# Nine products of a zeroed tile, x and a table asked for in another order, and the first filter pairs signed and turned elsewhere in a filter-and-experts kernel

## The chip, the cores and the metric

The kernel runs on one core of one Trainium2 chip. Its time is device time in microseconds, from five executions: the median is 475.29 (473.47 to 477.4). A sixth execution was taken with the hardware profiler; views of it are called the profile or the trace. The engines are PE (TensorE: matmuls and transposes), DVE (VectorE), ACT (ScalarE), POOL (GpSimd) and SP (SyncE, which here only issues DMAs). ACT and POOL issue DMAs too.

## The reference

What is computed, cut to what matters:

```python
# x: (8, 2496, 256); filt_r, filt_i: (1249, 256)
X = np.fft.rfft(x, axis=1)
y = np.fft.irfft(X * (filt_r + 1j * filt_i)[None], n=2496, axis=1)
t = y.reshape(19968, 256)                       # tokens
logits = t @ w_gate                             # 8 experts
expert = logits.argmax(1); p = softmax(logits)  # the gate of a token is p of its expert
out = zeros
for e in range(8):                              # the 80 tokens of highest gate are kept
    keep = top 80 of the tokens with expert == e
    out[keep] = gate[keep] * (relu(t[keep] @ w1[e]) @ w2[e])
```

## The kernel before, in words

The real transform of length 2496 = 39 x 64 is done as matrix products in float32, one sequence after another. Sequences are numbered b = 0 to 7.

- `load_x(b, ch)` (line 293) brings a chunk of x, 468 KB (the last of a sequence 234 KB), six chunks to a sequence, by SP's queue into one of NX0 = 7 buffers. Number 6b + ch gives the order of the chunks; chunk n takes the buffer of chunk n - 7, so its load waits until stage 1 has read that one.
- `stage1(b, k)` (302), eleven blocks k to a sequence, two blocks to a chunk: products with the table `wf_t` on PE into a PSUM tile `pa` (L309), copied by ACT into `t1` (L315). Here a block is 8 PE instructions in the profile.
- `transpose1(b, u)` (317), u = 0 to 9: four transposes of `t1` into `pt` (L323), copied by ACT to `t2` (L325). It needs all of the sequence's `t1`.
- `stage2(b, u)` (329): products with piece u // 2 of the table `d_t` into `pb` (L334); DVE multiplies by the two halves of the filter, `ft[0]` and `ft[1]` (two L342), POOL adds and subtracts the parts (two L348).
- `turn(b, u)` (352): products with `gi`, which holds an identity and the gate weights, into `py` (L357); ACT copies the spectrum out (L373) and stores it every second time (`yf`), DVE adds up the gate part `z` (L379, L380).

The filter is brought once, in ten rows of pairs: `load_filter(v, half)` (268) issues two indirect DMAs on POOL (L271), real part (half 0) or imaginary part (half 1) of pair v, v = 0 to 4. The row list `frow` is loaded by ACT's queue at the start. `sign_filter(v)` (276) turns the sign of imaginary rows on ACT (two L279), `turn_filter(v, k)` (282) transposes four tiles of half k on PE into a PSUM tile `pf` (L287), and DVE copies it into `ft[k]` (L289). `ft` of pair v serves the stage 2 of steps 2v and 2v + 1.

PSUM is dealt out in rings: `fps` has three buffers that `pa`, `pt` and `pb` take in turn; `pkps` has one buffer, in which `pf` lies; `yps` has two for `py`. A tile waits until the buffer's last reader is done.

The order of the work is written out by hand (lines 791 to 907): each engine and each queue runs its own instructions in the order in which this part of the program emits them, and waits only for data, for buffers and, for a DMA, for earlier landings. It emits

1. the loads of `frow`, `wf_t`, `fsig` by ACT's queue; on SP's queue the six chunks of sequence 0, piece 0 of `d_t` (`load_d(0)`), the first chunk of sequence 1; on POOL the gathers of filter pair 0, fills of zeros, the identities of `gi`, a copy `mark` of one element of the last chunk of sequence 0 (L826), which makes POOL wait for that chunk, then the gathers of pairs 1 and 2, with the gate weights (two small DMAs, L828 and L829) between the halves of pair 1;
2. eleven blocks of stage 1 of sequence 0; after each finished chunk the next load of x is issued (`put_x` in `put_s1`), and pieces 1 to 3 of `d_t` after blocks 2, 5 and 8;
3. the signing of pair 0, both its halves turned, `transpose1` of steps 0 and 1, each with a block of sequence 1, then piece 4 of `d_t`;
4. steps v = 0 to 81, v = 10b + u: `stage2(v)`; in steps 0 to 7 the signing (odd v) and turning of half v % 2 of pair v // 2 + 1; gathers of pairs 3 and 4 in steps 0 to 3; `transpose1` of step v + 2; a block of stage 1 (two where u = 3); a store of zeros to the output from step 10 on; `turn` of step v - 2.

After the last step come the gathers of the chosen tokens' rows, the choice itself, and the experts' two layers with their weights.

Of the kernel before, what the change touches and what calls it, by code (L numbers as in the profile page):

```python
# [13 lines left out]
F32 = mybir.dt.float32  # L14
BF16 = mybir.dt.bfloat16
# [8 lines left out]
B, S, C = 8, 2496, 256  # L24
# [3 lines left out]
NU = NS // 2  # L28
# [4 lines left out]
NCH = -(-NG // JC)  # L33
# [3 lines left out]
E, FF = 8, 1024  # L37
NDB, NFC = C // 128, FF // 128
# [43 lines left out]
def kernel(  # L82
# [11 lines left out]
    nc = tc.nc  # L94
# [9 lines left out]
                                  name=f"rows{h}_tbl") for h in range(2)]  # L104
# [5 lines left out]
    consts = ctx.enter_context(tc.tile_pool(name="consts", bufs=1))  # L110
    dpool = ctx.enter_context(tc.tile_pool(name="dram", bufs=1, space=DRAM))

    ident = consts.tile([128, 128], F32, name="ident")
    make_identity(nc, ident)
    ident_bf = consts.tile([128, 128], BF16, name="ident_bf")
# [63 lines left out]


    NE, NY, NO = 3, 2, 3
    yf = {b: dpool.tile([128, NS, C], F32, name=f"yf_{b}") for b in range(B)}
    ypool = ctx.enter_context(tc.tile_pool(name="spec", bufs=NY))
    ysb = {}
# [49 lines left out]
    with ExitStack() as actx:  # L234
# [6 lines left out]
        NX0 = 7  # L241
# [4 lines left out]
        fps = pool("fps", 3, PSUM)  # L246
        yps = pool("yps", 2, PSUM)
        pkps = pool("pkps", 1, PSUM)
# [12 lines left out]
        gi = tpool.tile([128, 2, ZW], F32, name="gi")  # L261
        ft = [tpool.tile([128, NU, NDB, 2, NQ], F32, name=f"ft{i}") for i in range(2)]

        st = {}
# [11 lines left out]
        def sign_filter(v):  # L276
            f = fst[:, v]
            for i in range(2):
                nc.scalar.activation(out=f[:, 2 + i, :], in_=f[:, 2 + i, :], func=AF.Copy,  # L279
                                     scale=fsig[:, 2 * v + i:2 * v + i + 1])  # L280

        def turn_filter(v, k):
            f = fst[:, v]
            ps = pkps.tile([128, 2, NDB, 128], F32, name=f"pf_{k}_{v}", tag="k")
            for i in range(2):
                for cb in range(NDB):
                    nc.tensor.transpose(ps[:, i, cb, :],  # L287
                                        f[:, 2 * k + i, 128 * cb:128 * cb + 128], ident[:])
            nc.vector.tensor_copy(  # L289
                out=ft[k][:, 2 * v:2 * v + 2].rearrange("p u c s q -> p u c (s q)"),  # L290
                in_=ps[:])

        def load_x(b, ch):
            xt = xpool.tile([128, JC, C], F32, name=f"x_{b}_{ch}", tag="x")
            ng = min(JC, NG - JC * ch)
            nc.sync.dma_start(
                out=xt[0:NJ * N1, 0:ng, :],
                in_=bass.AP(tensor=x.tensor, offset=x.offset + (b * S + JC * ch) * C,
                            ap=[[N2 * C, N1], [(NG - 1) * C, NJ], [C, ng], [1, C]]))
            st["x", b, ch] = xt  # L300
# [491 lines left out]
        with tc.manual_schedule():  # L792
            nc.scalar.dma_start(out=frow, in_=frow_dram.ap())
            nc.scalar.dma_start(out=wf_t, in_=wf_dram.ap())
            nc.scalar.dma_start(out=fsig, in_=fsig_dram.ap())
            xs = [(b, ch) for b in range(B) for ch in range(NCH)]
            s1 = [(b, k) for b in range(B) for k in range(NB)]

            def put_x():
                if xs:  # L800
                    load_x(*xs.pop(0))

            def put_s1():
                if s1:
                    b, k = s1.pop(0)
                    stage1(b, k)
                    if (2 * k + 2) % JC == 0 or k == NB - 1:
                        put_x()

            def load_d(g):  # L810
                nc.sync.dma_start(out=d_t[:, SG * g:SG * g + SG, :],
                                  in_=d_dram.ap()[:, SG * g:SG * g + SG, :])

            for _ in range(NCH):
                put_x()
            load_d(0)
            for _ in range(NX0 - NCH):
                put_x()
            load_filter(0, 0)
            load_filter(0, 1)  # L820
            for t in (lg, zero_t, *zs, key, kt):
# [1 line left out]
            nc.gpsimd.tensor_copy(out=gi[:, 0, 0:128], in_=ident[:])  # L823
            nc.gpsimd.tensor_copy(out=gi[:, 1, 0:128], in_=ident[:])
            mark = tpool.tile([1, 1], F32, name="mark")
            nc.gpsimd.tensor_copy(out=mark[:], in_=st["x", 0, NCH - 1][0:1, 0, 0:1])  # L826
            load_filter(1, 0)
            nc.gpsimd.dma_start(out=gi[:, 0, 128:128 + E], in_=moe_w_gate[0:128, :])  # L828
            nc.gpsimd.dma_start(out=gi[:, 1, 128:128 + E], in_=moe_w_gate[128:256, :])  # L829
            load_filter(1, 1)  # L830
            load_filter(2, 0)
            load_filter(2, 1)
            for k in range(NB):
                put_s1()
                if k in (2, 5, 8):
                    load_d(k // 3 + 1)
            sign_filter(0)
            turn_filter(0, 0)
            turn_filter(0, 1)
            for v in range(LEAD):  # L840
                transpose1(0, v)
                put_s1()
            load_d(4)
            nlow = max(128 - cap, 8) // 8
            n0 = max(128 - cap, 8) // 8
            early = {67: [lambda: pick_edge(0, 6, 8, -1.0)],
# [17 lines left out]
            for v in range(B * NU + LATE):  # L864
                b, u = divmod(v, NU)
                if b < B:
                    stage2(b, u)
                    if v + 2 < NU:
                        if v % 2 == 1:
                            sign_filter(v // 2 + 1)  # L870
                        turn_filter(v // 2 + 1, v % 2)
                    if v < 4:
                        load_filter(3 + v // 2, v % 2)
                    elif v == 4:
                        nc.gpsimd.dma_start(out=e_t, in_=e_dram.ap())
                        nc.gpsimd.dma_start(out=wi_t, in_=wi_dram.ap())
                    w = v + LEAD
                    if w < B * NU:
                        transpose1(*divmod(w, NU))
                    put_s1()  # L880
                    if u == 3:
                        put_s1()
                    if b > 0:
                        put_zeros(1)
                if v >= LATE:
                    turn(*divmod(v - LATE, NU))
                if b > 0 and u == LATE:
                    logits(b - 1, 0)
                if b > 0 and b % 2 == 0:
                    if u == LATE + 1:  # L890
                        logits(b - 1, 1)
                    if b < 6 and u in (4, 5, 6, 7, 8, 9):
                        gating(b // 2 - 1, u - 4)
                        if u == 9:
                            gating(b // 2 - 1, 6)
                    elif b == 6 and u in (4, 5):
                        gating(2, 2 * u - 8)
                        gating(2, 2 * u - 7)
                    elif b == 6 and u in (6, 7):
                        gating(2, u - 2)  # L900
                        if u == 7:
                            gating(2, 6)
                for act in early.pop(v, []):
                    act()
                if v == B * NU + 1:
                    turn_rows(0, 0)
                    turn_rows(0, 1)
# [663 lines left out]
```

## Time and profile before

| | us |
|---|---|
| median of five executions | 475.29 |
| lowest, highest | 473.47, 477.4 |
| the profiled execution | 474.33 |
| its span, first to last instruction | 472.5 |
| PE busy in 0:20, 20:40, 40:60, 60:80 of the span | 12.84, 15.72, 19.62, 20.00 |
| ACT busy in the same stretches | 10.95, 11.11, 13.49, 13.62 |
| DVE busy | 3.05, 9.12, 10.20, 9.18 |
| POOL busy | 11.21, 16.65, 10.70, 8.48 |
| share of the DMA engines' time in use | 0.81, 0.91, 0.61, 0.66 |

A line of a view names the start and length in us (in the timeline), the engine, the line of the kernel, the operation, the tiles written <- read, the shape, and how many of them were merged (x8). In square brackets stands how long the engine sat idle before it and what ended that. In the table of waits a line reads: who waited <- for whom: us in total, times, longest. PEld is PE's loading of weights, which overlaps its products.

### The profile page before, as it was taken

What the parts mean: (1) busy time and instruction counts of PE and PEld (TensorE: products, weight loads), DVE (VectorE), ACT (ScalarE), POOL (GpSimd) and SP (SyncE); (2) the same over time, 40 slices, a digit from 0 to 9 for tenths busy, and PEclk for the clock granted to TensorE, in tenths of its full rate; (3) what the DMA queues carried; (4) which work ended last, traced back from release to release, by engine and by line L of the source; (5) the groups of instructions that cost most, each with busy time, mean ns of one, the idle gap of its engine ahead of it and who ended that gap; (6) DMA issues with size and microseconds to landing.
All of it is one profiled execution on the core that took longest, in us unless ns stands there. A gap on an engine that the chain in (4) does not pass through costs nothing. (4 is left out here: it accounts for less than half of the span.)

```text
span 472.5 us, 8669 instructions
## 1 busy us (share of the span) xinstructions
PE 433.6 (92%) x3380; PEld 408.2 (86%) x3380; DVE 185.5 (39%) x542; ACT 223.0 (47%) x364; POOL 184.2 (39%) x252
## 2 busy tenths in 40 slices
PE   4879999999999999999999998999939999999970
PEld 4769999999999999999999987888838888888850
DVE  2135544454664455664437984385200000110000
ACT  3747666666776766666667553322212231111110
POOL 7488343443543433543434549204560002113110
PEclk9999999999999999999999999999988999999995
DMA  7998467888778787788962225987857953998010
GB/s 200 255 268 273 132 193 250 243 253 251 263 235 254 272 279 242 206 275 259 388 258 83 104 120 192 362 323 291 326 171 305 378 207 104 376 389 294 7 28 2
DMA packets 39476, 109.95 MB, mean 233 GB/s; under 512 B 5073, under 2 KB 14608, under 8 KB 38658
## 3 DMA queue, kind: packets, MB, share of 16 engines
q1 hardware_dynamic: 28688, 76.41, 49.5%
q10 hardware_dynamic: 6178, 21.04, 11.3%
q0 software_dynamic: 4560, 11.86, 8.2%
q8 instruction: 29, 0.48, 0.4%
q14 instruction: 21, 0.17, 0.1%
HBM read 68.97 MB, written 43.20 MB: 237 GB/s over the span
## 5 line engine op out<-in xcount | busy, mean ns | idle before, releaser
L348 POOL TENSOR_TENSOR p<-p,p 128x256 f32<-128x256 f32 x160 | 114.2, 736 | 134.9 <-DVE p L342 107.2
L342 DVE TENSOR_TENSOR p<-pb,ft 128x512 f32<-128x512 f32 x160 | 102.2, 680 | 15.8 <-PE pb L334 15.7
L315 ACT COPY t<-pa 128x480 f32<-128x480 f32 x88 | 87.1, 1000 | 27.5 <-PE pa L309 27.4
L309 PE MATMUL pa<-wf_t,x 117*128 117x120 f32 x704 | 92.5, 279 | 7.2 <-DMA x<-in_x_dram 6.9
L309 PEld LDWEIGHTS pa<-wf_t,x 117*128 117x128 f32 x704 | 86.5, 195 | 7.6 <-DMA x<-in_x_dram 5.7
L357 PE MATMUL py<-gi,p 128*128 128x136 f32 x640 | 88.1, 280 | 2.3 <-POOL p L348 2.3
L334 PE MATMUL pb<-d_t,t 128*128 128x128 f32 x640 | 85.2, 276 | 0.2
L357 PEld LDWEIGHTS py<-gi,p 128*128 128x128 f32 x640 | 79.8, 190 | 2.9 <-POOL p L348 2.9
L334 PEld LDWEIGHTS pb<-d_t,t 128*128 128x128 f32 x640 | 78.0, 191 | 1.0 <-PE py L357 0.4
L325 ACT COPY t<-pt 128x512 f32<-128x512 f32 x80 | 46.9, 586 | 65.0 <-PE pt L323 64.2
L504 PE MATMUL po<-yb,wt 128*128 128x256 f32 x240 | 58.5, 389 | 7.6 <-issue 6.7
L504 PEld LDWEIGHTS po<-yb,wt 128*128 128x128 f32 x240 | 44.5, 195 | 13.4 <-issue 6.9
L323 PE MATMUL pt<-ident,t 128*128 128x128 f32 x320 | 48.0, 273 | 0.0
L497 ACT COPY wt<-pw 128x512 f32<-128x512 f32 x40 | 23.3, 586 | 52.4 <-PE pw L493 41.1
L379 DVE COPY z<-py 128x16 f32<-128x16 f32 x60 | 11.2, 186 | 91.7 <-ACT ysp L373 57.9
L323 PEld LDWEIGHTS pt<-ident,t 128*128 128x128 f32 x320 | 37.7, 142 | 0.0
L373 ACT COPY ysp<-py 128x512 f32<-128x512 f32 x60 | 35.4, 590 | 0.0
L1147 PEld LDWEIGHTS ph<-xs,w 128*128 128x128 f32 x256 | 29.7, 192 | 1.7 <-DVE xs L1138 1.1
L1147 PE MATMUL ph<-xs,w 128*128 128x80 f32 x256 | 29.8, 274 | 0.8 <-DVE xs L1138 0.8
L1162 PE MATMUL po<-w,hT 128*80 128x256 f32 x128 | 28.8, 379 | 0.0
L1117 POOL DMA_INDIRECT xg<-y_sel,idxg x8 | 7.7, 966 | 45.9 <-DMA y_sel<-yr 44.0
L1167 POOL DMA_INDIRECT out_dram<-ys,idxs x8 | 7.5, 934 | 46.1 <-ACT ys L1165 46.1
(195 smaller groups left out, 331.4 us busy)
## 6 DMA issues: line engine op xcount, KB each, us to landing
out_dram<-zero_t SPq DMA_DIRECT2D x64, 312.0 KB
x<-in_x_dram SPq DMA_DIRECT2D x40, 468.0 KB
w<-in_moe_w_dram SPq DMA_DIRECT2D x16, 1024.0 KB
yf<-ysp ACTq DMA_DIRECT2D x30, 512.0 KB
yb<-yf SPq DMA_DIRECT2D x6, 2560.0 KB
yf<-ys ACTq DMA_DIRECT2D x10, 512.0 KB
x<-in_x_dram SPq DMA_DIRECT2D x8, 234.0 KB
d_t<-d_tbl SPq DMA_DIRECT2D x5, 256.0 KB
```

What stands on the lines that cost most here:

```text
L309: nc.tensor.matmul(out=ps[:, i, :, 2 * NS * cb:2 * NS * cb + 2 * NS], lhsT=xt[0:NJ * N1, (2 * k + i) % JC, 128 * cb:128 * cb + 128], rhs=w ...
L315: nc.scalar.copy(out=t1[:, 2 * k - h:2 * k - h + 2], in_=ps[:])
L323: nc.tensor.transpose(ps[:, i, cb, :], t1[:, a:a + 2, :].rearrange("p r n -> p (r n)"), ident[:])
L325: nc.scalar.copy(out=t2[:].rearrange("p i c -> p (i c)"), in_=ps[:].rearrange("p i c q -> p (i c q)"))
L334: nc.tensor.matmul(out=ps[:, cb, i], rhs=d_t[:, 2 * u + i, :], start=True, stop=True, lhsT=t2[:, i, 128 * cb:128 * cb + 128])
L342: nc.vector.tensor_tensor(out=pt, in0=ps[:].rearrange("p c s r q -> p (c s) r q"), in1=f.unsqueeze(2).to_broadcast([128, 2 * NDB, 2, NQ]), ...
L348: nc.gpsimd.tensor_tensor(out=yt[:, :, r, :], in0=yt[:, :, r, :], in1=pr[1][:, :, 1 - r, :], op=op)
L357: nc.tensor.matmul(out=ps[:, i, ZW * cb:ZW * cb + ZW], rhs=gi[:, cb, :], lhsT=yt[:, 2 * cb + i].rearrange("p r q -> p (r q)"), start=True, ...
L373: nc.scalar.copy(out=dst.rearrange("p s (h w) -> p s h w", h=2), in_=pv[:, :, :, 0:128])
L504: nc.tensor.matmul(pos[t][:, 0, 0:C], lhsT=wts[t, g // 2][:, g % 2, i, :], rhs=ybs[t][:, s, :], start=(s == 0), stop=(s == NS - 1))
L1147: nc.tensor.matmul(ph[:, fc // 4, fc % 4, 0:cap], lhsT=self.w1s[e][:, k, 128 * fc:128 * fc + 128], rhs=xs[:, k, :], start=(k == 0), stop=( ...
L1162: nc.tensor.matmul(po[0:cap, :], lhsT=hT[:, fc, :], rhs=self.w2s[e][:, fc, :], start=(fc == 0), stop=(fc == NFC - 1))
```

## The change

- A tile `warm` of zeros, 128 x 128 in bfloat16, is filled on DVE first of all; nine products of it with itself, 512 columns wide, are put ahead of the first block on PE. They write a tile of the ring `fps` that nobody reads.
- The gate weights are loaded by ACT's queue, right after `fsig`, and no longer by POOL's.
- `mark` reads chunk 3 of sequence 0, no longer chunk 5.
- Pieces 1 to 4 of `d_t` are asked for after block 7 and in steps 0, 2 and 4; a dictionary `held` names for chunks 7 to 20 the step before which they are not asked for (-1: after block 7). This is a place in the order of emission. A chunk is also asked for only when an earlier one has been used up (`free`).
- The signing of pair 0 is emitted after block 6. Before the steps there is one block of sequence 1, not two; the other comes in step 7.
- In steps 0 to 7 the turning of a filter half moves from after `stage2` to after the block of stage 1. The imaginary halves lie in the ring `fps`, not in `pkps`.

```diff
+    warm = consts.tile([128, 128], BF16, name="warm")
+    nc.vector.memset(warm[:], 0.0)
...
+    NWARM = 9
...
         def turn_filter(v, k):
             f = fst[:, v]
-            ps = pkps.tile([128, 2, NDB, 128], F32, name=f"pf_{k}_{v}", tag="k")
+            ps = (fps if k else pkps).tile([128, 2, NDB, 128], F32, name=f"pf_{k}_{v}",
+                                           tag="f" if k else "k")
...
             nc.scalar.dma_start(out=fsig, in_=fsig_dram.ap())
+            for cb in range(NDB):
+                nc.scalar.dma_start(out=gi[:, cb, 128:128 + E],
+                                    in_=moe_w_gate[128 * cb:128 * cb + 128, :])
+            pre = fps.tile([128, 4, 128], F32, name="warm_ps", tag="f")
+            for _ in range(NWARM):
+                nc.tensor.matmul(out=pre[:], lhsT=warm[:], start=True, stop=True,
+                                 rhs=warm[:].unsqueeze(1).to_broadcast([128, 4, 128]))
...
-            def put_x():
-                if xs:
+            held = dict(zip(range(NX0, NX0 + 14),
+                            (-1, 0, 2, 3, 4, 5, 7, 8, 11, 13, 15, 16, 17, 18)))
+            free = [NX0]
+
+            def put_x(v):
+                while xs and free[0] and held.get(B * NCH - len(xs), -1) <= v:
                     load_x(*xs.pop(0))
+                    free[0] -= 1
 
             def put_s1():
                 if s1:
                     b, k = s1.pop(0)
                     stage1(b, k)
                     if (2 * k + 2) % JC == 0 or k == NB - 1:
-                        put_x()
+                        free[0] += 1
...
             for _ in range(NCH):
-                put_x()
+                load_x(*xs.pop(0))
             load_d(0)
             for _ in range(NX0 - NCH):
-                put_x()
+                load_x(*xs.pop(0))
+            free[0] = 0
...
-            nc.gpsimd.tensor_copy(out=mark[:], in_=st["x", 0, NCH - 1][0:1, 0, 0:1])
+            nc.gpsimd.tensor_copy(out=mark[:], in_=st["x", 0, NCH - 3][0:1, 0, 0:1])
             load_filter(1, 0)
-            nc.gpsimd.dma_start(out=gi[:, 0, 128:128 + E], in_=moe_w_gate[0:128, :])
-            nc.gpsimd.dma_start(out=gi[:, 1, 128:128 + E], in_=moe_w_gate[128:256, :])
             load_filter(1, 1)
...
             for k in range(NB):
                 put_s1()
-                if k in (2, 5, 8):
-                    load_d(k // 3 + 1)
-            sign_filter(0)
-            turn_filter(0, 0)
-            turn_filter(0, 1)
+                if k == 6:
+                    sign_filter(0)
+                if k == 7:
+                    load_d(1)
+                    put_x(-1)
+            for k in range(2):
+                turn_filter(0, k)
             for v in range(LEAD):
                 transpose1(0, v)
-                put_s1()
-            load_d(4)
+            put_s1()
...
                     stage2(b, u)
-                    if v + 2 < NU:
-                        if v % 2 == 1:
-                            sign_filter(v // 2 + 1)
-                        turn_filter(v // 2 + 1, v % 2)
+                    if v + 2 < NU and v % 2 == 1:
+                        sign_filter(v // 2 + 1)
+                    if v in (0, 2, 4):
+                        load_d(2 + v // 2)
+                    put_x(v)
...
                     put_s1()
-                    if u == 3:
+                    if u == 3 or v == 7:
                         put_s1()
+                    if v + 2 < NU:
+                        turn_filter(v // 2 + 1, v % 2)
```

## The prediction

> **What bounds the kernel now.** The page comes first: its busy table, then its 40 slices (11.8 us each).
>
> ```profile
> PE 433.6 (92%) x3380; PEld 408.2 (86%) x3380; DVE 185.5 (39%) x542; ACT 223.0 (47%) x364; POOL 184.2 (39%) x252
> ...
> PE   4879999999999999999999998999939999999970
> DMA  7998467888778787788962225987857953998010
> ```
>
> TensorE (PE) is full from slice 4 to slice 24, so until about 283 us the time is PE work plus the holes in the first 60 us. DMA is full in slices 2 and 3 and nearly idle (2) in slices 22 to 24, so no backlog is carried out of the main loop: what the start gains, the loop's end gains, and all later work hangs on that end. Next the PE timeline of the start:
>
> ```profile
> 5.66 5.63 PE L309 MATMUL pa<-wf_t,x 117*128 117x120 f32 x32 [5.66 <-DMA x<-in_x_dram]
> 11.56 2.02 PE L309 MATMUL pa<-wf_t,x 117*128 117x120 f32 x16 [0.27 <-ACT t L315]
> 14.81 4.85 PE L309 MATMUL pa<-wf_t,x 117*128 117x120 f32 x40 [1.24 <-DMA x<-in_x_dram]
> ...
> 21.08 0.83 PE L287 MATMUL pf<-ident,fst 128*128 128x128 f32 x4 [0.98 <-ACT fst L279]
> ```
>
> A block of stage 1 is 8 of these. Blocks 0 to 3 run from 5.66, 4 and 5 from 11.56, 6 to 10 from 14.81: the last two groups start when a chunk of x lands. The table by windows counts 18 products in the 3.80 us from 5.66 (0.211 us each), 16 in the 1.84 us after that (0.115). Its clock column reads 1.00 in both, but the spacing shows a PE at about half rate until 9.46. Third, the waits of PE from 15 to 60 us, and the stall at 28:
>
> ```profile
> PE pf L287 <- ACT fst L279: 2.5, 5, 1.0
> PE pf L287 <- issue: 2.1, 1, 2.1
> PE pa L309 <- DMA x<-in_x_dram: 1.2, 1, 1.2
> ```
> ```profile
> 19.35 0.95 POOL L271 DMA_INDIRECT fst<-in_filt_r_dram,frow  x1 [0.30 <-issue]
> ...
> 23.11 0.98 POOL L271 DMA_INDIRECT fst<-in_filt_i_dram,frow  x1 [0.30 <-issue]
> ...
> 28.00 0.44 PE L287 MATMUL pf<-ident,fst 128*128 128x128 f32 x2 [2.07 <-issue]
> ```
>
> After 19.67 PE waits for filters, not for x: for their signing on ScalarE (ACT), and at 28.00 for a gather issued at 19.35, 8.65 us earlier. Last, a step without a stall:
>
> ```profile
> 50.09 1.05 PE L334 MATMUL pb<-d_t,t 128*128 128x128 f32 x8
> 50.98 0.60 PE L287 MATMUL pf<-ident,fst 128*128 128x128 f32 x4
> 51.41 0.60 PE L323 MATMUL pt<-ident,t 128*128 128x128 f32 x4
> 51.85 1.05 PE L309 MATMUL pa<-wf_t,x 117*128 117x120 f32 x8
> 52.74 1.10 PE L357 MATMUL py<-gi,p 128*128 128x136 f32 x8
> 53.67 1.05 PE L334 MATMUL pb<-d_t,t 128*128 128x128 f32 x8
> ```
>
> From start to start: stage 2 0.89, a filter half 0.44, transposes 0.44, a block 0.89, the turn back 0.93; together 3.59.
>
> **The change, part by part.**
>
> *Nine products.* Before shows no bf16 product 512 wide. Below, one costs what a 120-wide one does, 0.211, so nine take 1.9; above, 512/120 x 0.211 = 0.90, so nine take 8.1. From about 1.2 us they end between 3.1 and 9.3. Even at 9.3 blocks 0 to 5 end by 14.9 (six at 0.92), when block 6 may start now. Their gain, were x there, is 3.80 x (1 - 0.115/0.211) = 1.7 us. But chunks 2 and 3 still open their groups at 11.56 and 14.81, since these loads are issued as before and first on SP's queue. I take 0, and keep -1.7 and +0.2. The memset (a like one on POOL takes 0.20) lies on an idle DVE.
>
> The Trainium skill, "TensorE: Matmul & The Clock Gate", Part 1, says that the clock doubles after a busy window of some 3.4 us; nine cold products of 512 columns at 1.2 GHz are an estimate of 3.8 us, enough. By the rule alone the sum would be 1.7 lower; the row of x's arrival says that this is waiting time.
>
> *Gate weights to ACT's queue.* POOL loses two issues, 20.31 to 21.50 and the gap to 21.80: 1.5 us between two gathers. ACT issues them instead (0.6 each) before its table load at 2.17; its first copy is at 7.75, so 0. If that cover went, 1.3.
>
> *The mark.* It waits for chunk 3 of x (PE takes it up at 14.81) and not chunk 5 (17.73): gathers of filter pair 1 start 3.0 us earlier (15.05, 16.3), its second half 4.2 (17.6, 18.9), later ones 4.2.
>
> *Signing pair 0 after block 6.* ACT copies blocks 6 to 10 back to back, 4.76 us from 15.97. Adding 0.89 there ends the last at 21.62, and the transposes, which need it, start at 21.65 instead of 21.75. So the PE wait of 0.98 becomes a wait for ACT: gain 0.1. Bounds: 0, and 0.98 if ACT catches up. Then transposes, one block, and stage 2 of step 0 at 23.4; before it was 24.40 with one block more (0.89), so 23.51 like for like.
>
> *SP's order.* Table pieces go ahead of x of sequence 1; nothing in the trace ties an SP issue to a step, only to a free buffer (136.0 us of waits on L309) or to an earlier landing (6.7 us). The chunk after d piece 1 is needed at 27.6 rather than 28.71; before it was queued ahead of that piece. The earlier gathers share with it: DMA gives 265 GB/s here; gathers of 131 KB, issued one per 1.27 us, can take up to 103 of it, so the 0.74 MB up to and with the chunk of block (1,0) take 0.74/0.162 = 4.6 us from 17.7: 22.3, needed at 22.5. I take 0; bounds -0.5 and +1.5.
>
> *Filters turned last in a step, imaginary halves in the ring `fps`.* Without stalls steps 0 to 7 are 2 x 2.66 + 4 x 3.59 + 2 x 4.48 = 28.6 with the block moved into step 7, 27.7 as before. Before took 57.85 - 24.40 = 33.45: 5.7 lost. What is late next:
> - pair 1 real: 16.3 + 8.65 = 25.0, turned at 25.65: hidden, 0.7 to spare.
> - pair 1 imaginary: the gather at 23.11 is signed at 31.48, 8.4 later; now 18.9 + 8.4 = 27.3, signed by 27.8, turned at 28.8: hidden. Behind the signing on ACT stand the copies of transposes and block.
> - later pairs: POOL does two gathers and two L348 in 4.0 us per step (29.19 to 32.99 to 36.82: 3.8); PE needs 3.6 to 4.9. They keep the 1 to 2 us to spare.
> - new wait: the ring has 3 buffers. In odd steps the imaginary half (or, in 3 and 7, the second block) takes the buffer that stage 2 filled three tiles before. DVE frees it after its two L342, 2.4 to 2.6 us after stage 2 began (37.22 to 39.67: 2.45), and PE is there after 2.22. So 0.3 in steps 1 and 5, 0.45 in 3 and 7 where DVE also has `z` to add, and 0.2 at the start of step 1: 1.7 in all. The turn back and the next stage 2 are queued behind it. Bounds: 0 and 3.0.
>
> Loop: 5.7 - 1.7 = 4.0. **Sum: 4.0 + 0.1 = 4.1 us.** The profiled execution took 474.33 (span 472.5, 1.8 outside): 470.2. The median, 475.29, lies 0.96 above it: 471.2.
>
> What lies behind should move as a whole: SP's wait of 50.6 us on L342 for a spectrum ends with the loop. A stretch at clock 0.83 (340 to 360 us) may fall otherwise, 20 x 0.17 = 3.4 us at most, which is luck of either sign.
>
> The skill's "DMA: Bandwidth & Descriptors", Queues, rings and completion order, has each DMA engine take turns between queues by packet, so gathers issued earlier slow the x transfers beside them. The sum above has that by the trace's own rates; by the rule with equal turns SP would have half of 265, that chunk would land at 23.3, and 0.8 of the gain would go.
>
> **The rivals.**
> - *More comes back*: DVE keeps up, the ring costs nothing (1.7 more), and ACT or x come a little earlier (0.7). Gain 6.5: 468.8. For it: DVE is busy 10.2 of 20 us in 40:60. Against: it stands behind ACT in `z` (57.9 us of waits).
> - *The filters stay late*: 2.0 us more from issue to use, since x, table and eight gathers now ask together. Steps 0 and 1 stall again: gain 2.0, 473.3, no change that can be told. For it: DMA at 0.91 in 20:40. Against: no byte is added.
> - *Slower, by x of sequence 2*: chunks 15 to 18 are asked for two steps (6.4 us) ahead of use in SP's order, where before it was eleven. If SP really stands at its step, behind zero stores and landings, and a chunk needs 8 us (as the gathers do), five chunks cost 1.6 each, 8.0, less 4.1: 479.2. It decides once issue to landing exceeds 6.4 us at 65 to 95 us. Against: DMA there is at 0.64 to 0.86, and SP waits for nothing of a step.
> - *Not what it says*: the clock is not released by the nine products. By the sum above the time is then the same, so its chance is in the forecast's.
>
> **How the numbers follow.** A measurement here tells 0.5% (2.4 us) from no change: 472.9 to 477.7 is the same. Forecast 471.2 (469.8 to 472.9): 0.57. More comes back: 0.19. Late filters: 0.15. Slower: 0.09. Faster is 0.57 + 0.19 = 0.76. The range leaves out the slower case and the outer edges of both neighbours: 468.0 to 474.2.
>
> **What would show it.** Right: products at 0.115 from the first x on, blocks 6 to 10 still opened near 14.8; step 0's stage 2 near 23.4; no hole before L287 at 25 to 31; stage 2 of step 8 near 53.8 instead of 57.85; small holes before L287 or L309 in odd steps, released by L342. Wrong: a wait of L309 on x after 20 us, POOL's L348 or ACT before PE in steps 0 to 7, or a tail that does not follow the loop's end.

## The result, and the profile after

The changed kernel takes 475.19 us (median of 43 runs, 469.53 to 478.24), the kernel before 476.11 (85 runs, 472.44 to 479.48): a ratio of 0.9965, 95% interval 0.9952 to 0.9979. The ratio compares executions in the faster of two states alone, so it is not the quotient of these medians. It stands for 1.7 us, less than the 0.5% that the prediction called no change. The forecast was 471.2, its range 468.0 to 474.2: wrong. The profiled execution of after took 475.36, with a span of 473.5; that of before, 474.33, lies 1.8 under its median here, so the two traces side by side show the places, and not the 1.7 us.

The page of after, its busy table, PE's 40 slices (11.8 us each), the granted clock and DMA, and below it the clock of before:

```profile
PE 438.1 (93%) x3389; PEld 411.3 (87%) x3389; DVE 186.2 (39%) x543; ACT 223.0 (47%) x364; POOL 182.7 (39%) x250
...
PE   7779999999999999999999998999959999999970
...
PEclk9979999999999999999999999999988999999995
DMA  7989885488788887787962235997857962999000
```
```profile
PEclk9999999999999999999999999999988999999995
```

New is the clock of the third slice, 24 to 35 us: 7 tenths, where before has 9. PE is at 7 there in both. The table by windows, before from 20 to 30 us and then after from 20 to 40 (columns: stretch, length, busy time of PE, PEld, DVE, ACT, POOL, then clock, DMA share, GB/s):

```profile
20.00:30.00 10.00, 6.91 (x57) 6.21 (x57) 3.36 (x5) 4.91 (x8) 8.07 (x11) 1.00 0.93 269
```
```profile
20.00:30.00 10.00, 4.84 (x27) 4.37 (x26) 1.38 (x2) 3.02 (x4) 3.34 (x4) 0.74 0.90 262
30.00:40.00 10.00, 10.00 (x84) 10.00 (x84) 6.17 (x11) 6.33 (x10) 7.29 (x9) 0.91 0.90 249
```

In 20 to 30 us PE ran 27 instructions; before it ran 57. The start on PE's timeline is near what the prediction said it would be:

```profile
0.99 3.79 PE L805 MATMUL warm_ps<-warm 128*128 128x512 bf16 x9 [0.99 <-DVE warm L114]
6.22 4.11 PE L313 MATMUL pa<-wf_t,x 117*128 117x120 f32 x32 [1.44 <-DMA x<-in_x_dram]
11.34 2.02 PE L313 MATMUL pa<-wf_t,x 117*128 117x120 f32 x16 [1.01 <-ACT t L319]
```

The products end at 4.78, the first block starts when x lands (at 6.22, before 5.66), and blocks 6 to 10 run from 14.27. Then comes what it did not say. The waits of PE from 15 to 60 us, in place of the filter waits:

```profile
PE pa L313 <- DVE ft L293: 2.9, 1, 2.9
PE pt L327 <- issue: 2.3, 1, 2.3
```

And the timeline of all engines from 17 to 28 us:

```profile
19.28 1.04 PE L291 MATMUL pf<-ident,fst 128*128 128x128 f32 x8
...
20.81 0.94 POOL L274 DMA_INDIRECT fst<-in_filt_r_dram,frow  x1 [0.30 <-issue]
21.61 0.96 ACT L319 COPY t<-pa 128x480 f32<-128x480 f32 x1 [1.96 <-PE pf L291]
22.05 0.95 POOL L274 DMA_INDIRECT fst<-in_filt_i_dram,frow  x1 [0.30 <-issue]
...
24.39 0.69 DVE L293 COPY ft<-pf 128x512 f32<-128x512 f32 x1 [19.94 <-PE pt L327]
25.83 0.69 DVE L293 COPY ft<-pf 128x512 f32<-128x512 f32 x1 [0.74 <-remote]
26.57 1.57 PEld L313 LDWEIGHTS pa<-wf_t,x 117*128 117x128 f32 x7 [3.09 <-DVE ft L293]
```

Read it by what is missing. PE's last block ended at 19.46 and its two filter halves at 19.90 and 20.33, yet ACT copies that block only at 21.61 and DVE the halves at 24.39 and 25.83, though both were idle. The semaphore events in the trace say why: PE's signals came at 21.54, 24.37 and 25.81, some 2 to 5.5 us after the products (whose ends the profile models; that ACT and DVE stood idle it measures). PE's own next products need these copies, so it stands from 20.32 to 22.63 and from 23.72 to 26.57. During the second idle stretch the granted clock falls to half, 24.9 to 31.7. Stage 2 of step 0 starts at 28.43 (before 24.40, predicted 23.4), of step 8 at 58.77 (before 57.85, predicted 53.8). In between no step stalls, and the tail after the last stage 2 is 184.2 us long in both: it follows the loop, as predicted.

### The profile page after: what moved, and what is told of

It reads as the page before. It is cut to its first block, busy times and chain, and to the rows that moved or that the text cites. A ratio compares the mean times of both kernels' runs of the same rounds, so it can differ in the third digit from the quotient of the medians.

```text
span 473.5 us, 8679 instructions
## 1 busy us (share of the span) xinstructions
PE 438.1 (93%) x3389; PEld 411.3 (87%) x3389; DVE 186.2 (39%) x543; ACT 223.0 (47%) x364; POOL 182.7 (39%) x250
## 5 line engine op out<-in xcount | busy, mean ns | idle before, releaser
L508 PE MATMUL po<-yb,wt 128*128 128x256 f32 x240 | 60.1, 397 | 6.7 <-issue 3.9
L508 PEld LDWEIGHTS po<-yb,wt 128*128 128x128 f32 x240 | 45.5, 199 | 12.9 <-issue 4.1
## 6 DMA issues: line engine op xcount, KB each, us to landing
x<-in_x_dram SPq DMA_DIRECT2D x40, 468.0 KB
```

The lines of the kernel that those rows point to most:

```text
L508: nc.tensor.matmul(pos[t][:, 0, 0:C], lhsT=wts[t, g // 2][:, g % 2, i, :], rhs=ybs[t][:, s, :], start=(s == 0), stop=(s == NS - 1))
```

## Experiments: the parts of the change

The runs fell on five chips, in groups of three or four kernels that share a chip and its runs of the kernel before. On three chips that kernel takes 465.8 to 466.2 us, on two 475.7 to 476.6, as in the result. I call them 466-chips and 476-chips; ratios are against before on the same chip. The first two groups ran on 466-chips.

**The change without its nine products** (466-chip).

```diff
-    warm = consts.tile([128, 128], BF16, name="warm")
-    nc.vector.memset(warm[:], 0.0)
...
-            pre = fps.tile([128, 4, 128], F32, name="warm_ps", tag="f")
-            for _ in range(NWARM):
-                nc.tensor.matmul(out=pre[:], lhsT=warm[:], start=True, stop=True,
```

> The whole change without the nine products and their tile. In the profile of the changed kernel PE's signal for block 10 came at 21.5 us though its products were issued by 19.45, those for the two filter halves at 24.4 and 25.8, and the clock then fell to half until 31.7: stage 2 of step 0 began at 28.43 where I had worked out 23.4. Theory P (the nine products shift PE's own code by 18 instructions, so that a load of code falls into this crowded stretch): without them stage 2 of step 0 begins by 24.5, no half clock at 25 to 32, ratio about 0.990 to before. Theory G (the gathers, moved forward by the mark, crowd that stretch): no better, 28 us again, ratio 0.996 or 1.7 us above that, as the clock is cold for the first blocks.

461.06 us, ratio 0.9894 [0.9853, 0.9935]; step 0 at 22.19, step 8 at 52.24. No signal of PE is late.

**The mark on chunk 5 again** (466-chip).

```diff
-            nc.gpsimd.tensor_copy(out=mark[:], in_=st["x", 0, NCH - 3][0:1, 0, 0:1])
+            nc.gpsimd.tensor_copy(out=mark[:], in_=st["x", 0, NCH - 1][0:1, 0, 0:1])
```

> The whole change, but the mark reads chunk 5 again, so the gathers of pairs 1 and 2 start at about 17.5 and not at 14.5. Theory G: the late signals of 19.5 to 25.8 go or shrink to under 1 us, stage 2 of step 0 begins near 24, but pair 1 comes 3 us later and PE waits 1 to 2 us for it in step 0; ratio 0.990 to 0.994. Theory P: the signals are as late as in the changed kernel, step 0 at 28 or later, ratio 0.997 or above.

461.78, ratio 0.9927 [0.9889, 0.9964]; step 0 at 21.86, then a wait of 1.2 for the gather of a later filter half, step 8 at 52.73.

**The gate weights on POOL again** (466-chip).

```diff
-                nc.scalar.dma_start(out=gi[:, cb, 128:128 + E],
...
             load_filter(1, 0)
+            nc.gpsimd.dma_start(out=gi[:, 0, 128:128 + E], in_=moe_w_gate[0:128, :])
+            nc.gpsimd.dma_start(out=gi[:, 1, 128:128 + E], in_=moe_w_gate[128:256, :])
```

> The whole change, but the gate weights are loaded by POOL's queue again, between the halves of pair 1. In the changed kernel chunk 4 of x was asked for at 6.19 us and no longer at 4.40, and the first block began at 6.22 and not 5.66. Theory Q (the two small transfers ahead of x cost the start): first block at 5.66 again, 0.5 us gained; else nothing changes. Theories G and P: within 0.3 per cent of the changed kernel, late signals as before.

462.39, ratio 0.992 [0.9891, 0.9949]; step 0 at 22.28, step 8 at 51.73.

**The kernel before with the nine products alone** (466-chip).

```diff
+            pre = fps.tile([128, 4, 128], F32, name="warm_ps", tag="f")
+            for _ in range(9):
+                nc.tensor.matmul(out=pre[:], lhsT=warm[:], start=True, stop=True,
```

> The kernel before with the nine products alone. As predicted: no gain, since chunks 2 and 3 of x open their blocks at 11.5 and 14.8 in any case; ratio 0.998 to 1.002, products of block 0 at 0.115 us. Theory P: the shift of PE's code by 18 instructions makes or moves a stall in 19 to 30 us, ratio up to 1.006.

464.91, ratio 0.9983 [0.9953, 1.0012]: nothing that can be told, as predicted. Step 0 at 23.25, step 8 at 56.73, with before's stall of 2.07 ahead of step 1, here followed by half clock from 28.0 to 31.4. The four runs differ little, and every one that holds most of the change gains: the result's stall was not there to be taken away. So the change itself was run again.

**The change, unaltered** (another 466-chip).

> The changed kernel, nothing left out or altered. With the products alone, the gates or the mark put back, PE's signals were on time (block 10 within 0.01 us), step 0's stage 2 began at 21.9 to 22.3 and step 8's at 51.7 to 52.7. Theory V (the late signals of 19.5 to 25.9 belong to that one execution or its chip): here signals on time, step 0 near 22.3, step 8 near 52, ratio 0.992 or less. Theory K (they belong to the whole change: the products with the gates on ACT's queue and the early mark together): late again, step 0 at 26 to 28, half clock at 25 to 32, ratio 0.996 or more.

459.77, ratio 0.9859 [0.9819, 0.99]: 6.4 us. PE's timeline:

```profile
14.06 4.92 PE L313 MATMUL pa<-wf_t,x 117*128 117x120 f32 x40 [0.55 <-DMA x<-in_x_dram]
18.82 1.04 PE L291 MATMUL pf<-ident,fst 128*128 128x128 f32 x8
20.32 1.09 PE L327 MATMUL pt<-ident,t 128*128 128x128 f32 x8 [0.46 <-ACT t L319]
...
22.14 1.06 PE L338 MATMUL pb<-d_t,t 128*128 128x128 f32 x8
```

This is the size of the rival "more comes back" (gain 6.5): no wait at all for a filter, transposes at 20.32, step 0 at 22.14, step 8 at 50.91. From the first filter product to the transposes it takes 1.50 us (18.82 to 20.32), before 2.25 (19.50 to 21.75; the same on a 466-chip with the products alone), so the early signing is worth 0.75. The rest of the lead over 21.65 is x: blocks 6 to 10 opened at 14.06 and not 14.81. ACT shows how it can be:

```profile
16.01 0.89 ACT L282 ACTIVATE fst<-fst,fsig 128x256 f32<-128x256 f32 x2
16.80 3.47 ACT L319 COPY t<-pa 128x480 f32<-128x480 f32 x4
```

Four copies in 3.47, each 0.98 long: (3.47 - 0.98) / 3 = 0.83 from start to start, since they overlap. So ACT can catch up after the signing, which the prediction kept only as a bound.

**Turning back at its old place** (same chip): right after stage 2, both halves in `pkps`.

```diff
+                    if v + 2 < NU:
+                        turn_filter(v // 2 + 1, v % 2)
                     if v in (0, 2, 4):
...
-                    if v + 2 < NU:
-                        turn_filter(v // 2 + 1, v % 2)
```

> The whole change, but each filter half is turned right after stage 2 again and all lie in pkps. I predicted that turning last costs up to 1.7 us in the ring and hides the waits for the filters. Theory T (the place of the turning hides most of the wait): with the place undone PE waits 1 to 2 us in step 0 and 0.6 in each odd step, step 8 begins 3 to 5 us later than in the changed kernel on this chip, ratio 0.998 or so. Rival M (the earlier gathers do it, by the mark and the gates): step 8 at most 1 us later.

462.1, ratio 0.9927 [0.9891, 0.9963]. PE waits 1.1 us for signings and 0.8 for `ft`; step 8 at 53.98 instead of 50.91. Turning last is worth 2.3 us by the medians, 3.1 by step 8 (the intervals of the two ratios just overlap).

**SP's old order** (same chip): no `held` list; table pieces after blocks 2, 5, 8 and at the end.

```diff
-                while xs and free[0] and held.get(B * NCH - len(xs), -1) <= v:
+                while xs and free[0]:
...
-                if k == 7:
-                    load_d(1)
-                    put_x(-1)
+                if k in (2, 5, 8):
+                    load_d(k // 3 + 1)
```

> The whole change, but x and the table pieces are asked for in SP's order of the kernel before: a chunk as soon as an earlier one is used up, pieces 1 to 3 after blocks 2, 5 and 8, piece 4 before step 0. Theory as predicted (the order is worth nothing): step 8 within 0.5 us of the changed kernel, ratio within 0.2 per cent. Rival O (the order lets the filters land sooner): gathers of pair 1 land 1 to 2 us later, PE waits for them in steps 0 and 1, step 8 later by 1 to 2 us.

459.34, ratio 0.9844 [0.9809, 0.9879], as good as the change: the order is worth nothing.

**No products, and gate weights on POOL** (same chip): the first and the third edit together.

> The change without the nine products and with the gates on POOL's queue: only the mark, the order, the signing and the turning are left. Without the products the ratio was 0.989, with the gates on POOL 0.992. If both the products and the gates on ACT cost a little, this is the best of all: ratio 0.987 to 0.989, first block at 5.7. If they cost nothing it equals the changed kernel on this chip within 0.2 per cent.

460.71, ratio 0.988 [0.9842, 0.9918], 0.9 from the change, inside both intervals.

## Experiments: what happened in the result

The third group ran on a 476-chip, and the stretch was back in every kernel that has the change.

**The change once more** (476-chip).

> The change unaltered once more, to learn whether the stretch from 19.5 to 31.7 us of the result's profile (PE idle twice, 5.2 us in all, then half clock) belongs to the change or to the chip that it ran on. If it belongs to the change under some chance at the start: stage 2 of step 0 at about 28 in this profile too, and a ratio near 0.996. If the two earlier looks at this kernel are the rule: step 0 at 22.1, step 8 at 50.9, ratio 0.982 to 0.990. On a chip where the kernel before takes 476 instead of 466 the first is to be expected, on one with 466 the second.

474.77, ratio 0.9974 [0.9947, 1.0]. PE idle 2.44 at 22.14 and 2.23 at 25.46, half clock 24.9 to 31.7, step 0 at 27.32, step 8 at 58.20: the result's profile again. The stretch belongs to the kind of chip.

**Without the products, beside it** (same chip): the first edit again.

> The change without its nine products, this time beside the change on the same chip. If the products do nothing (they end before x is there): within 0.5 us of the change, step 0 within 0.2 us of it. If the products cost what they delay (the first block started 0.3 to 0.5 us later with them): 0.5 us faster. If the clock that they release is worth what the prediction kept as its bound: 1.7 us slower. On a chip with the late stretch: if the products bring it about, step 0 at 22 here and 28 in the change; if not, 28 in both.

474.96, ratio 0.9977 [0.9943, 1.0012]; step 0 at 28.61, step 8 at 58.20. The products neither bring the stretch about nor matter.

**Pair 0 signed after block 10** (same chip).

```diff
-                if k == 6:
-                    sign_filter(0)
...
+            sign_filter(0)
             for k in range(2):
                 turn_filter(0, k)
```

> The change with the signing of filter pair 0 back behind block 10, as before; all else as in the change. The prediction's theory (ACT copies blocks 6 to 10 back to back, so signing earlier only moves the same work): the first filter half 0.1 us later and the time 0.1 us longer. The rival, from the profile after (ACT's copies start 0.80 to 0.87 us apart instead of 0.95, so it catches up): the wait of 0.98 in front of the first filter half comes back, step 0 starts 0.8 to 1.1 us later than in the change, and the time is 0.8 to 1.1 us longer.

473.68, ratio 0.9966 [0.9938, 0.9993]. PE waits 3.3 ahead of the second filter half; step 0 at 26.67. The late signals cover what was to be measured: it does not tell the two theories of the signing apart. That the early signing is worth 0.75 us rests on the rows of the change on a 466-chip.

**The kernel before with turning last alone** (same chip).

```diff
-                        turn_filter(v // 2 + 1, v % 2)
...
+                    if v + 2 < NU:
+                        turn_filter(v // 2 + 1, v % 2)
```

> The kernel before with one part of the change alone: filters turned last in a step, imaginary halves in the ring fps. The prediction gave the loop's gain of 4.0 us to later turning and earlier gathers together. If turning last is what counts: the stall at 28 goes or shrinks to 1, the waits for signing go, and the loop gains 3 to 4 us: ratio 0.991 to 0.994. If the gathers' start counts as much: the first imaginary half, landing at 31.5 as before, is still waited for in steps 1 to 3, and the gain is 1 to 2 us: ratio 0.996 to 0.998. The ring's new wait, 1.7 us by the prediction, would show in odd steps as waits for DVE's products; in the change none did.

473.21, ratio 0.9959 [0.9937, 0.9981]. Its gathers start at 17.8 and not 14.0, and so do its late signals: none over 0.5 before 24, then ACT or DVE start 1.4 to 4.3 us late from 24.5 on. Step 0 starts at 24.36 in time, step 1 only at 30.85, step 8 at 57.66. So with the gathers in their old place readers are held up on this chip too, one step later.

Here the pattern showed. I compared, in every trace, the end of each PE product that signals with the next event on its semaphore. By itself this misleads: for 440 or 441 such signals in a program the traces of 476-chips up to here hold 424 to 432 events, those of 466-chips 441 to 443, and where an event is missing the next one looks late. So the reader has to be asked as well. A signal counts as late below where the engine that reads the product stood idle, with nothing of its own in the way, and started over 0.3 us after the product's end (0.04 is usual); the largest in each stretch, beside POOL's gathers there:

```
                        start      loop       rest of     tail: gathers at    305-307  334-351  390-393
                                              the loop    286-296
result, before (476)    0.55       none       none        none                none     6.7      none
result, after (476)     5.5        none       none        none                none     10.0     none
change again (476)      5.0        0.35       none        none                none     7.1      none
change again (466)      none       none       none        none                none     none     none
gathers: before         18 ...................44          in all kernels as headed, a few us
         change         14-24      32-46                  earlier or later
```

On the 476-chips readers start more than 1 us late only during or shortly after a row of gathers: those of the start and the fourteen of 334 to 351. Beside the pairs of the loop they are 0.8 us late at the most, in any of the traces. Nor does every row do it: that of before, at 18 to 28, costs 0.55. On 466-chips, in eleven profiles, no reader waits beside the same rows. I first read the missing events as late signals too, hence the theory G: on these chips PE's signals are held up whenever gathers are issued. The rival T: by the traffic, whoever asks for it.

**Plain loads in place of the gathers** of pairs 1 to 4 (another 476-chip), as many bytes, on POOL's queue as well. The rows are not the filter's, so this kernel leaves the right filters out, and the routing behind the loop takes 1,100 us more; only the profile up to 280 us is read for the start.

```diff
+                if v:
+                    r = min(128 * (2 * v + i), 1121)
+                    nc.gpsimd.dma_start(out=fst[:, v, 2 * k + i, :], in_=filt[r:r + 128, :])
+                    continue
                 nc.gpsimd.indirect_dma_start(
```

> The change, with the indirect gathers of filter pairs 1 to 4 replaced by plain loads of as many bytes from POOL's queue (the rows are then not the filter's own, so the output leaves the right filters out; nothing else differs). Theory G: on the chip of the result's kind (kernel before at 476) PE's signals come late while POOL issues gathers, and only then: 14 to 24 and 32 to 46 us in the change. Without gathers there: signals on time from 10 to 280 us, stage 2 of step 0 at 22 instead of 27 to 28, ratio 0.984 to 0.990, while the late signals at 293, 306 and 334 to 351 us stay, where the gathers of the routing stay. Theory T, the traffic itself is what delays them: step 0 at 27 or more as before, ratio 0.996 to 0.999. On a chip of the other kind (before at 466): step 0 at about 22 either way, ratio 0.984 to 0.988, and nothing is told apart.

PE's timeline:

```profile
19.50 1.04 PE L295 MATMUL pf<-ident,fst 128*128 128x128 f32 x8
20.99 1.09 PE L331 MATMUL pt<-ident,t 128*128 128x128 f32 x8 [0.46 <-ACT t L323]
...
22.81 1.06 PE L342 MATMUL pb<-d_t,t 128*128 128x128 f32 x8
```

Step 0 at 22.81, with the 466-chip's small wait of 0.46 and a full clock; DMA moved 264 GB/s in 10:20 and 265 in 20:30, no less than in after (254 and 262). No signal is late from 10 to 280 us, and no event is missing there. Behind the loop, where the routing's fourteen gathers stayed, readers start up to 10 us late as ever. T falls, and the stretch at the start is shown to come with the gathers. What in them does it is not: the plain loads are also a shorter row, POOL issuing them from 14.8 to 19.1 and not from 14 to 24. Up to step 7 (47.07) the loop runs 0.7 behind the 466-chip's; then ACT stands 4 us at a store of the spectrum, as it did for 3 us on a 466-chip without the products, and step 8 starts at 53.76. Its ratio was not to be had, since the tail is another.

**Gathers added**, two in every other step from 20 to 42, into a tile nobody reads (same chip).

```diff
+                    if 20 <= v < 44 and v % 2 == 0:
+                        for i in range(2):
+                            nc.gpsimd.indirect_dma_start(
+                                out=dum[:, v % 4 + i, :], out_offset=None, in_=bass.AP(
```

> The change with 24 more gathers, two in every other step from 20 to 42 (about 89 to 165 us), into a tile that nobody reads. Theory G on a chip of the result's kind: PE's signals, on time there in the change, come 0.4 us or more late at most of the twelve pairs. Theory T and every theory by which the late signals belong to the start of the program: on time there. Time: POOL's own products are put off by 2.5 us at each pair, which by their spare time of 1 to 2 us costs 0 to 1 us each, so up to 12 us on any chip; the lateness under G adds 5 to 20 us more on the one chip. On a chip of the other kind no signal is late.

473.27, ratio 0.9932 [0.9903, 0.9962]. At six of the twelve pairs (at 107, 123, 130, 142, 156 and 175 us) the next event comes 0.9 to 1.9 us after a product; the readers show that it is an event missing, and no signal late. At the first of them the event after the product that ends at 107.96 is at 109.83, yet ACT, which stood idle for it, starts at 107.99:

```profile
106.99 0.97 POOL L892 DMA_INDIRECT dum<-in_filt_r_dram,frow  x1
...
107.36 0.60 PE L327 MATMUL pt<-ident,t 128*128 128x128 f32 x4
...
107.99 0.59 ACT L329 COPY t<-pt 128x512 f32<-128x512 f32 x1 [0.91 <-PE pb L338]
```

No idle reader at any of the twelve pairs starts late, and PE has no wait from 90 to 180 us. So what G forecast did not come, nor the 5 to 20 us of cost, and G as I had worded it falls: pairs of gathers delay nothing here. What the traces leave is narrower: rows of gathers do. A row of eight in the middle of the loop, which would tell this from something that belongs to the start, was not run; the fourteen of the tail speak for the row.

**Pair 2 gathered in the loop** (same chip), four gathers ahead of it instead of eight.

```diff
-            load_filter(2, 0)
-            load_filter(2, 1)
...
-                    if v < 4:
-                        load_filter(3 + v // 2, v % 2)
+                    if v < 6:
+                        load_filter(2 + v // 2, v % 2)
```

> The change with only four gathers (pair 1) ahead of the loop instead of eight: those of pair 2 move to steps 0 and 1, pairs 3 and 4 to steps 2 to 5. Theory G on a chip of the result's kind: the late stretch ends some 5 us earlier, after the fourth gather at 18 instead of the eighth at 23.3, and stage 2 of step 0 starts at 23 to 25 instead of 27 to 28: ratio 0.987 to 0.993. Theory T: as the change, 0.996 to 0.998. On a chip of the other kind: pair 2 lands at about 31 and is turned at 32 to 35, so 0 to 2 us slower than the change, ratio 0.986 to 0.990.

The late signals end at 21.4 instead of 25.5, and step 0 starts at 24.28 instead of 27.3; behind this row of four the readers start 1.5 us late at the most. So the shorter row costs less. The time is 478.94 all the same, ratio 1.0044 [1.002, 1.0069], because now the filters are late; its waits of PE from 15 to 60 us:

```profile
PE pf L291 <- DMA fst<-in_filt_r_dram,frow: 4.0, 2, 3.4
PE pf L291 <- ACT t L329: 3.3, 1, 3.3
```

The last three were to show whether another place for the gathers keeps the gain on a 476-chip; they ran on a third 466-chip, with no late signal, and only tell what each place costs there.

**The mark on chunk 5 once more**: the second edit.

> The change with POOL's mark back on chunk 5 of x, so that the eight gathers start at about 17 instead of 14; all else as in the change. On a chip of the result's kind, theory G (signals late while gathers issue): the late stretch moves to 19 to 28, so blocks 6 to 10 and the first filters are on time; step 0 starts at 23 to 25 instead of 27 to 28, but steps 0 and 1 are then held up: step 8 at 56 to 58, ratio 0.994 to 0.998, no better than the change. If what counts is that the start itself is spared: ratio 0.990 or less. On a chip of the other kind: 0.9927, as in the first look.

461.57, ratio 0.9902 [0.987, 0.9935]; waits of 1.2 and 0.8 for filters, step 8 at 54.12.

**No mark**: the gathers follow POOL's fills at once.

```diff
-            mark = tpool.tile([1, 1], F32, name="mark")
-            nc.gpsimd.tensor_copy(out=mark[:], in_=st["x", 0, NCH - 3][0:1, 0, 0:1])
```

> The change without the mark: the eight gathers start as soon as POOL has cleared its tiles, at 11.8 instead of 14. Theory G on a chip of the result's kind: the late stretch ends 2.2 us earlier (23.5 instead of 25.7) and step 0 starts at 25 to 26, ratio 0.992 to 0.995, unless x comes later by the bytes taken (0.5 MB of gathers ahead of chunk 5, up to 2 us), which would eat it up: 0.997. On a chip of the other kind: 0 to 2 us slower than the change.

460.78, ratio 0.9884 [0.9843, 0.9926]; step 0 at 23.55, since x comes later.

**Gathers of pairs 1 and 2 right behind those of pair 0**, ahead of the fills, without the mark.

> The change with the gathers of pairs 1 and 2 right behind those of pair 0, ahead of POOL's clearing of tiles: 8.0 to 18 instead of 14 to 24. Theory G on a chip of the result's kind: the late stretch falls into the time in which PE waits for x anyway and ends at about 19.5; step 0 starts at 22.5 to 24, ratio 0.985 to 0.991, if x is not late; 1.05 MB of gathers at 265 GB/s take 4.0 us from x, so at the worst step 0 at 26 and ratio 0.996. On a chip of the other kind x's delay alone counts: 0 to 4 us slower than the change, ratio 0.986 to 0.995.

461.75, ratio 0.9908 [0.9879, 0.9938]; step 0 at 24.77: the gathers cost x 2.6 us.

## Why the prediction was wrong, step by step

- **The nine products, 0**: right, and so is its reason, that x opens blocks 6 to 10 (at 14.27 in after, 14.06 on the 466-chip). But that they release the clock holds only half of the time: it was granted by 5.4 us in eight of the fifteen profiles with them, in the other seven at 9.7 to 12.7, as without them (9.5 to 12.1). The unaltered change had it at 4.41 in the result and at 10.02 on the 466-chip, where it gained 6.4.
- **Gate weights to ACT's queue, 0**: right within what was measured.
- **SP's order, 0**: right (0.9844 against 0.9859). No wait for x of sequence 2 came; the rival "slower" fell.
- **Signing pair 0 early, 0.1**: mis-sized. "Back to back" was taken as 0.95 a copy; ACT can start one every 0.83. It is worth 0.75 on a 466-chip, inside the bounds of 0 and 0.98.
- **The ring's new wait, 1.7**: did not come, neither there nor in after. I had the imaginary half wait for DVE. In the trace its first product (27.03 in step 1) waits for signals of ACT, whose copy of the transposes ends at 26.93; it is the next stage 2, at 27.47, that waits for DVE's products, and these end at 27.19. The buffers change hands in another order than I worked out, and neither waits.
- **Filters hidden, tail follows**: right; no PE wait for a filter in the change on a 466-chip, and the same tail length on the result's chip.
- **The mark: "gathers of filter pair 1 start 3.0 us earlier", at no cost but their share of DMA.** This is the step that failed. The times were right (14.52, predicted 15.05). The price of the gathers was taken from bytes alone, and on the result's chip it was paid elsewhere: eight gathers in a row now ran beside blocks 6 to 10 and the first filters, where PE, ACT and DVE wait for one another's signals at once, and readers started up to 5.5 us late. Step 0 began 6.3 us later than on the 466-chip (28.43 against 22.14): PE idle 5.2 and not 0.5, the filters 0.5 later, the rest half clock. With plain loads in place of the gathers step 0 began at 22.81 on such a chip. Putting the mark back alone was not run on a 476-chip, and turning last with the gathers in their old place gained no more there (step 8 at 57.66); so it is the price of a row of gathers that is shown to be missing from the sum, and not that its old place was free.

On a 466-chip the gain of 6.4 us is there, more than the forecast's 4.1; the signing (0.65 more) and the ring (1.7 more) would make 6.45, but before was not profiled on such a chip, so this split is not shown. On 476-chips most of the gain is taken back at the start: step 8 of the change stands 7.9 us behind that of the 466-chip (58.77 against 50.91), while before stands 1.1 behind before with the products alone (57.85 against 56.73).

The profile of before held the clue, and I passed it by as "luck of either sign". Its timeline of all engines, 345 to 355 us:

```profile
349.71 0.99 POOL L476 DMA_INDIRECT gts<-rows_tbl,idxb  x1 [0.30 <-issue]
...
350.68 0.37 ACT L509 COPY yr<-po 128x256 f32<-128x256 f32 x1 [5.72 <-remote]
...
354.13 1.22 PE L504 MATMUL po<-yb,wt 128*128 128x256 f32 x2 [6.70 <-issue]
```

PE idle for 6.7 us with no releaser, ACT idle for 5.7, fourteen gathers in a row beside them (334 to 351): the same thing, in the kernel before.

What stays open: why a row of gathers holds PE's signals up on some chips and not on others, by what path, and why the row of before cost little. Not shown either: a kernel with the right output and the full gain on a 476-chip; turning last alone (0.9959) and the change (0.9974) can't be told apart there.

## What to carry to other kernels

When work is moved earlier, look in the profile of before for what happens beside that kind of work elsewhere: an idle stretch put down to "issue" or "remote" beside it is a price that bytes do not show. On the chips that showed it, rows of gathers did harm, while 24 more in pairs in the middle of the loop delayed no reader; so gathers are better spread out in pairs, early enough for their data. A kernel that does so and keeps the whole gain was not run. When an event looks late, ask the reader too: a trace can lack the event. And one chip is one sample: the same change was 0.986 on one and 0.997 on another.

## What was not expected of the hardware

- Chips differ by 2% for the same kernel (466 against 476), and most of it sits in few places: the tail after the last stage 2 is 184.2 us in before on the result's chip, 176.5 on a 466-chip (before with the products alone). The late signals of up to 6.7 us beside the tail's row of gathers lie in that stretch.
- Signals of PE, from products that had been issued on time, came up to 5.5 us late beside a row of eight indirect gathers, while plain loads of as many bytes from the same queue left them on time. The Trainium skill, "SBUF — State Buffer", section "SBUF: two separate sides", says that a DMA and a compute operation cannot slow each other, since their ports are disjoint. The run with plain loads agrees as to the bytes; the gathers did delay compute on these chips, by a path that the runs don't show.
- Two idle stretches of PE, 2.3 and 2.9 us, with 1.1 of work between, were followed by 6.8 us at half clock, which began during the second. The skill's "TensorE: Matmul & The Clock Gate", Part 1, has the clock watched in windows of some 3.4 us and halved after an idle one; 6.8 is two of them, and the trace shows that no single idle stretch of that length is needed. With the products alone on a 466-chip one of 2.07 was enough for 3.4 us at half clock, and before, on its own chip, kept its clock after one as long.
